# First batch's key and query transposes two rounds later, and the fourth sum of each group behind its first channel products

## The chip, the core and the metric

The kernel runs on one core of a Trainium2 chip. The metric is the device time of one execution in microseconds (us); a comparison uses medians of several executions. The engines that matter are TensorE (PE in the profile, with its weight loads as PEld), VectorE (DVE), ScalarE (ACT), GpSimd (POOL, which here mostly starts loads) and SyncE (SP, which starts transposing transfers and stores). Each engine runs its own instructions in program order; they wait for each other through semaphores.

## The reference

Two stages follow each other. The shapes are batch 8, 12 heads, 448 tokens, head size 64, so a token has 768 channels.

```python
scores = scale * np.matmul(q, k.transpose(0, 1, 3, 2)) - np.log(S)
attn = 1.0 / (1.0 + np.exp(-scores))
x = np.matmul(attn, v)                       # then heads side by side: (8, 448, 768)
h = np.maximum(x.T @ w_tok1, 0.0) @ w_tok2   # tokens mixed, 448 -> 256 -> 448
u = x + h.T
out = u + np.maximum(u @ w_ch1, 0.0) @ w_ch2 # channels mixed, 768 -> 1536 -> 768
```

The attention is a sigmoid without a sum over a row, so a round of scores can be used as soon as its sigmoid is done.

## The kernel before

**Units and groups.** Batches 0 and 1 are the units A and B and are done one at a time; the other six form the groups 1, 2 and 3 of two batches each (lines 73 to 81). A unit has three pairs, a group six; a pair is a set of four heads' worth of rows that fill the 128 partitions. `(A, 1)` is the second pair of unit A.

**A pair's attention** takes seven rounds j = 0 to 6. `scores` (line 442) does four small matmuls into one of two PSUM pair banks, then ACT computes the sigmoid of 128x896 into the tile `attn` (line 456). The two banks alternate, so the matmuls of round n+2 wait until the sigmoid of round n is over. `values_mm` (line 462) multiplies a round's `attn` by the values. For unit A each round's value product comes on its own (`value_step`, line 1404); after j = 6 two DVE casts bring the result to SBUF (line 1412), and then follow, per pair: eight transposes back to rows (`back`, line 500, copy at line 506), eight matmuls of the first token product (`tok1_third`, line 639), and two times two of the second (`tok2_third`, line 671, added by DVE at line 680). The second needs the token weights in order, one DVE copy of 128x896 (line 1355, `tokens_turned`).

**Keys and queries** must be transposed. For the pairs of A, of B and the first of group 1 TensorE does it: `turn_by_pe` (line 369) issues 14 small transposes (line 376) into a free bank of m2 and m3 and one DVE copy of 128x896 (line 381), once for k and once for q. All later pairs are turned by a GpSimd copy and a transposing transfer on SP (lines 363 and 391).

**The channel products.** Units A and B use plain products (lines 887 and 945). A group uses seven products in place of eight for each 2x2 block (as Winograd does): `ch1_pieces` (line 728) has 42 pieces of three matmuls each (line 768), in the order p = 1, 2, 6, 5, 7 of column block 0, then 1 and 2 of block 1, 4 of block 0, 6 of block 1, and 3 of block 0. Pieces 1, 6 and 7 go one after another into the same bank m0, m1 or m2 and each is copied out by DVE before the next is added (`save`, line 783, for group 3 partly by ACT at line 781). Piece 5 reads the sum S1, piece 6 S2, piece 7 S3 and piece 3 S4. `ch1_sum` (line 706) makes them on DVE at line 722 from the transposed rows `uT`; S1 and S2 come in parts, S3 (in place, in `uT`) and S4 as one 128x1344 instruction each.

**What sets the order.** While the program is written, a plan keeps a clock for each engine (`clock`) and the time at which each result will be there (`there`). `first_attention` (line 1347) takes for TensorE, among its candidates, the one that can start first; a tie goes to the one that is listed first: scores, the next entry of `quick` (back and token products), the next entry of `turns` (TensorE's transposes), the copy of the token weights, a value step, then B's rounds. `one` (line 1128) puts the two transposes of the next pair in `turns` after a given round. `merge` (line 1249) does the same for all that follows: channel products in their fixed order (`main`), attention and token work spread between them (`sec`), sums for DVE (`side`). An entry of `side` may be written once the position in `main` has reached its first number; `base[g]` is the position of group g's first piece. Loads from GpSimd are planned by `pool_dma` (line 171): 0.61 an issue, a time of flight, and a cost on a clock of the load path.

Of the kernel before, what the change touches and what calls it, by code (L numbers as in the profile page):

```python
# [21 lines left out]
def kernel(  # L22
# [58 lines left out]
    PAIRS = [(u, i) for u in UNITS for i in range(NPAIR[u])]  # L81
    BY_PE = 7
# [15 lines left out]
    AROUND = ("B", 1, 2, 3)  # L98
    BEHIND = 0.0
    WARM = 9  # L100
    BANKS = ("m0", "m1", "m2", "m3")
    AWAY = 1
    ORDER = (4, 5, 6, 3, 0, 1, 2)
# [22 lines left out]
    clock = {"pe": 1.0, "dve": 1.0, "act": 1.0, "pool": 1.0, "sp": 1.0, "load": 2.4}  # L126
    there, held = {}, set()
# [23 lines left out]
    def did(engine, cost, needs, gives, tail=0.0):  # L151
        t = max([clock[engine]] + [there.get(key, 0.0) for key in needs])
        clock[engine] = t + cost
        for key in gives:
            there[key] = t + cost + tail
            held.discard(key)
        return t
# [12 lines left out]

    def pool_dma(issues, cost, needs, gives):
        did("pool", 0.61 * issues, needs, [])
        clock["load"] = max(clock["load"], clock["pool"] + 1.5) + cost
        for key in gives:
            there[key] = clock["load"] + 0.1

    hook, later = [], []

# [81 lines left out]
    def load_first():  # L260

        got = []
        for n, (j0, j1) in enumerate(KEYS):
            t = pa.tile(
                [128, 2, j1 - j0, E],
                FP16 if n else FP32,
                tag="pk" if n else "h2T",
                bufs=1 if n else 2,
                name=f"k_A_0{n}",
            )  # L270
            for side, (b, h) in enumerate(SIDES["A"]):
                engine = nc.gpsimd if n else nc.scalar if side else nc.sync
                engine.dma_start(
                    out=t[64 * side : 64 * side + 64, :, :, :],
                    in_=k[b, h : h + 2].rearrange("h (p j) e -> p h j e", j=J)[:, :, j0:j1, :],
                )
            got.append(t)
            if n:
                pool_dma(2, 0.2 * (j1 - j0), [], [("made", n)])
            else:  # L280
                did("sp", 0.56, [], [("raw", "A", 0, "k")], 2.9)
                clock["load"] += 0.2 * (j1 - j0)
                load("A", 0, "q")
        return got
# [84 lines left out]
    def turn_by_pe(g, i, what):  # L369
        at = either()  # L370
        t = turned(g, i, what)
        ps = bank(f"t{what}_{g}_{i}", [128, J, 2, P], FP16, at)
        m = raws[(g, i, what)]
        for j in range(J):
            for h in range(2):
                nc.tensor.transpose(  # L376
                    out=ps[64 * h : 64 * h + 64, j, :, :].rearrange("d b p -> d (b p)"),
                    in_=m[:, h, j, :],
                    identity=ident[:, :],
                )  # L380
        nc.vector.tensor_copy(out=t[:, :, :, :], in_=ps[:, :, :, :])
        m = f"m{at}"
        pe(0.42, [("raw", g, i, what), m], ["pe"], "col")
        dve(0.56, ["pe"], [(what, g, i), m])

    def turn_by_dma(g, i):
        for what in ("k", "q"):
            permute(g, i, what)
            m = linear[(g, i, what)]
            t = turned(g, i, what)  # L390
            nc.sync.dma_start_transpose(
                out=t.rearrange("e j b p -> e j (b p)"),
                in_=m.rearrange("p j h e -> p (j h e)"),
            )
            did("sp", 1.4, [("linear", g, i, what)], [(what, g, i)], DMAT)
        if later and later[0][0] <= clock["sp"] + BEHIND:
            later.pop(0)[1]()

    def ahead(g, i, n):
        at = PAIRS.index((g, i)) + n  # L400
        return PAIRS[at] if at < len(PAIRS) else None
# [3 lines left out]
    def load_next(g, i):  # L405


        if not ahead(g, i, 2) or PAIRS.index((g, i)) + 3 < BY_PE + 1:
            return
        def keys():  # L410
            t = state["turned"]
            return [("k", *ahead(g, i, 2))] + ([("uT", t, LAST)] if t is not None else [])

        def f():
            gate = pa.tile([1, 2], FP16, tag="gate", bufs=2, name=f"gate_{g}_{i}")
            last = max(keys(), key=lambda key: there[key])
            if last[0] == "k":
                source = kT[last[1:]][0:1, 0, 0, 0:2]
            else:
                source = uTs[last[1]][0:1, NDB - 1, 128 * LAST : 128 * LAST + 2]  # L420
            nc.gpsimd.tensor_copy(out=gate[:, :], in_=source)  # L421
            did("pool", 0.2, keys(), ["gate"])
            if ahead(g, i, 3):
                load(*ahead(g, i, 3), "k")
                load(*ahead(g, i, 3), "q")
            if PAIRS.index((g, i)) + 2 > BY_PE:
                load(*ahead(g, i, 2), "v")

        loads.append((keys, f))
# [12 lines left out]
    def scores(g, i, j):  # L442
        ps = pair_bank(f"qk_{g}_{i}_{j}", [128, 2, 512])
        at = pa.tile([128, 2, S], FP16, tag="attn", bufs=ATTN, name=f"attn_{g}_{i}_{j}")
        attn[(g, i, j)] = at
        for b in range(2):
            for h in range(2):
                r = slice(64 * h, 64 * h + 64)
                nc.tensor.matmul(  # L449
                    out=ps[64 * b : 64 * b + 64, h, 0:S],  # L450
                    lhsT=keys_of(g, i, j)[r, b, :],
                    rhs=qT[(g, i)][r, :, b, :],
                    start=True,
                    stop=True,
                )
        nc.scalar.activation(  # L456
            out=at[:, :, :], in_=ps[:, :, 0:S], func=SIGMOID, bias=att_bias, scale=att_scale
        )
        pe(0.2, [key_of(g, i, j), ("q", g, i), rot["at"]], ["pe"], "quad")
        act(0.83, ["pe"], [("attn", g, i, j), rot["at"]])  # L460
# [500 lines left out]
    def bank2(p, n):  # L961
        return {2: 3, 5: 2, 3: 2}.get(p, (1, 0, 1)[n])
# [159 lines left out]
    turns, quick, side, base = [], [], [], {}  # L1122
# [5 lines left out]
    def one(g, i, j):  # L1128
        scores(g, i, j)
        at = ahead(g, i, 1)  # L1130
        if j == (3 if (g, i) == ("A", 0) else 1) and at and PAIRS.index(at) < BY_PE:
            for what in ("k", "q"):
                turns.append(
                    ([("raw", *at, what), "m2/m3"], lambda what=what: turn_by_pe(*at, what))
                )
        after = ahead(g, i, 2)
        if j == J - 1 and after and PAIRS.index(after) >= BY_PE:
            keys = [("raw", *after, "k"), ("raw", *after, "q")]
            loads.append((lambda: keys, lambda: turn_by_dma(*after)))
            load_next(g, i)  # L1140
# [108 lines left out]
    def merge(main, sec):  # L1249
# [18 lines left out]
        def free(keys):  # L1268
# [3 lines left out]
            soon = [key for x in main[pos : pos + AWAY] for key in x[2]]  # L1272
            return not any(key in soon for key in keys if key in BANKS)

# [140 lines left out]
    with tc.manual_schedule(engines=None):  # L1415
        if WARM:
            zero = pa.tile([128, 512], FP16, tag="tmp", bufs=4, name="zero")
            nc.vector.memset(zero[:, :], 0.0)
            ps = pp.tile([128, 2, 512], FP32, tag="q1", bufs=1, name="warm")
            for _ in range(WARM):  # L1420
                nc.tensor.matmul(
# [3 lines left out]
        first = load_first()  # L1425
# [13 lines left out]
        load_pair("A", 2)  # L1439
        w_tok2_s = load_tok_weights()  # L1440
        pool_dma(3, 3.7, [], ["wtok"])
        load_pair("B", 0)

# [66 lines left out]
        for g in (1, 2, 3):  # L1510
# [13 lines left out]
            for m in range(42):  # L1524
                p, cb = chain_order(KC)[m]
                at = {2: 3, 5: (cb - 1) % 3, 3: (cb - 1) % 3}.get(p, cb % 3)
# [5 lines left out]
            for m in range(1, 25):  # L1532
# [3 lines left out]
                else:  # L1536
                    n, p = (m - 4) // 7, (1, 2, 6, 5, 7, 3, 4)[(m - 4) % 7]
                    at = bank2(p, n)
# [54 lines left out]
            (3, 0, S, (0, 1, 2), ("S1",), "S3"),  # L1593
        )
        for g in (1, 2, 3):
            first = base[g] - 8
            for m, c0, c1, blocks, after, gives in SUMS:
                needs = [("uT", g, t) for t in blocks] + [(x, g) for x in after]
                side.append(
                    (  # L1600
                        first,
                        first + 1000,
                        needs,
                        lambda g=g, m=m, c0=c0, c1=c1, needs=needs, gives=gives: ch1_sum(
                            g, m, c0, c1, needs, [(gives, g)]
                        ),
                    )
                )
        for m in range(16):
            made = base["B"] + NCB  # L1610
            first = made if m % 4 == 3 else base["A"] + 2
            side.append((first, made + (10 if m % 4 == 3 else 0), ["w1"], w_sum(m)))
        for m in range(12):
            first = base["A"] + NCB + J if m % 4 < 2 else made
# [38 lines left out]
```

## Time and profile before

| quantity | value |
|---|---|
| four runs | 365.4, 365.99, 366.58, 368.55 us; median 366.28 |
| the profiled execution | 365.4 us, of which its span from first to last instruction is 363.6 |
| TensorE | 351.6 us busy (97% of the span), 3113 matmuls |
| VectorE | 232.1 us (64%) |
| ScalarE | 197.5 us (54%) |
| GpSimd | 130.7 us (36%) |
| granted TensorE clock | 0.996 of full speed |

The profiled execution is the fastest of the four, and the runs spread by 3.15 us, which is 0.9%. A "wait" in the profile is idle time of an engine with the instruction that ended it. The chain of waits goes back from the last instruction, at each step to whatever released it. The table by stretches gives the busy time of each engine between two moments, so that the difference from the stretch's length is idle time. In a line of the timeline the first number is the start and the second the length in us; lines that follow each other closely can overlap by the time that a matmul takes to drain.

### The profile page before, as it was taken

To read this page: it belongs to the slowest core of one execution; us is meant where nothing else is said; L and a number is where in the kernel's file an instruction comes from. 1 tells how busy PE (TensorE), PEld (TensorE's weight loads), DVE (VectorE), ACT (ScalarE), POOL (GpSimd) and SP (SyncE) were. 2 spreads that over 40 slices of the span, in tenths; PEclk is the share of its full clock that TensorE was granted. 3 is DMA by queue.
4 is the path that set the end of the run, shared out by engine and by line. 5 is a ranking of instruction groups with operands and counts; after the bars stand their busy time and mean duration, and the time that the engine had idled before them with its cause. 6 is when DMAs were issued, how large, how long until landed. Compare 5 with 4: busy or idle time off the path is not lost.

```text
span 363.6 us, 7773 instructions
## 1 busy us (share of the span) xinstructions
PE 351.6 (97%) x3113; PEld 182.5 (50%) x3113; DVE 232.1 (64%) x435; ACT 197.5 (54%) x242; POOL 130.7 (36%) x211
## 2 busy tenths in 40 slices
PE   7899999999999999999999999999999999999994
PEld 3454555555544556444445556444445556455562
DVE  2467757666755588886654659666644588655862
ACT  4987266466765432387887743477887351342000
POOL 9982422465556610055655340066610000004000
PEclk9999999999999999999999999999999999999998
DMA  7999999689998946798999889998963158300153
GB/s 113 187 192 192 148 208 183 103 127 160 161 147 134 138 73 107 191 154 133 147 146 140 144 172 127 219 138 133 142 103 70 52 89 180 92 2 0 45 159 103
DMA packets 86725, 47.76 MB, mean 131 GB/s; under 512 B 60961, under 2 KB 82977, under 8 KB 86689
## 3 DMA queue, kind: packets, MB, share of 16 engines
q0 software_dynamic: 24288, 21.83, 41.3%
q1 hardware_dynamic: 61696, 23.96, 34.1%
q10 hardware_dynamic: 704, 1.48, 1.1%
q8 instruction: 24, 0.39, 0.4%
q14 instruction: 13, 0.10, 0.1%
HBM read 43.84 MB, written 11.01 MB: 151 GB/s over the span
## 4 chain that ended last, share of the span: by engine, by line
PE 89%; ACT 3%; DVE 2%; POOL 1%; DMA 1%; issue 1%; ACTq 0%; POOLq 0%
PE x L768 12%; PE x L1031 9%; PE qk L449 9%; PE xa L467 7%; PE z L768 6%; PE c_B L945 4%; PE z L1031 4%; PE k L538 4%; PE c_B L887 4%; PE yn L574 4%; PE c_A L887 4%; PE c_A L945 3%; PE d L1088 3%; PE y L1031 2%; PE y L768 2%; ACT attn_A L456 2%
## 5 line engine op out<-in xcount | busy, mean ns | idle before, releaser
L456 ACT ACTIVATE attn<-qk 128x896 f16<-128x896 f32 x126 | 110.5, 915 | 54.4 <-PE qk L449 47.1
L768 PEld LDWEIGHTS <-w 128*128 128x128 f16 x378 | 35.0, 98 | 39.1 <-issue 9.8
L449 PE MATMUL qk<-qT,kT 64*64 64x448 f16 x504 | 40.8, 363 | 0.6 <-ACT attn L456 0.6
L783 DVE COPY c<-x 128x448 f32<-128x448 f32 x42 | 26.1, 622 | 22.2 <-PE x L768 19.5
L768 PE MATMUL x<-uT,w 128*128 128x448 f16 x162 | 37.8, 353 | 0.1
L788 DVE CUSTOM_DVE_ANT_0 h2T<-z,c 128x448 f16<-128x448 f32 x36 | 22.5, 625 | 16.9 <-PE z L768 14.7
L224 ACT ACTIVATE u<-u 128x768 f16<-128x768 f32 x21 | 17.7, 844 | 24.7 <-DVE u L584 21.0
L252 POOL DMA_DIRECT2D k<-in_k_dram x36 | 21.4, 602 | 25.6 <-PE tk L376 12.1
L1043 DVE TENSOR_TENSOR u<-u,x 128x384 f32<-128x384 f32 x36 | 19.9, 552 | 16.3 <-PE x L1031 16.2
L1031 PEld LDWEIGHTS <-h2T 128*128 128x128 f16 x216 | 20.8, 98 | 15.0 <-issue 1.6
L363 POOL COPY pk<-k 128x896 f16<-128x896 f16 x17 | 16.3, 958 | 30.8 <-DMA k<-in_k_dram 30.8
L449 PEld LDWEIGHTS <-kT 64*64 64x64 f16 x504 | 13.7, 104 | 27.0 <-issue 25.1
L467 PE MATMUL xa<-attn,v 64*64 64x448 f16 x504 | 27.0, 350 | 0.0
L421 POOL COPY gate<-kT 1x2 f16<-1x2 f16 x16 | 2.8, 174 | 67.0 <-DMA kT<-pk 67.0
L456 ACT ACTIVATE attn_B<-qk_B 128x896 f16<-128x896 f32 x21 | 18.3, 917 | 15.4 <-PE qk_B L449 14.9
L768 PE MATMUL z<-s,w 128*128 128x448 f16 x108 | 24.6, 353 | 0.0
L688 POOL TENSOR_TENSOR r<-h2T,h2T 128x512 f16<-128x512 f16 x1 | 1.1, 1150 | 60.1 <-ACT h2T L236 60.1
L584 DVE TENSOR_TENSOR u<-x_nat,yn 128x384 f32<-128x384 f16 x42 | 21.2, 550 | 2.3 <-PE yn L574 2.1
L252 POOL DMA_DIRECT2D v<-in_v_dram x36 | 22.2, 644 | 0.3 <-issue 0.3
L252 POOL DMA_DIRECT2D q<-in_q_dram x36 | 21.8, 624 | 0.3 <-issue 0.2
L1031 PEld LDWEIGHTS <-r 128*128 128x128 f16 x162 | 15.5, 98 | 11.0 <-issue 1.2
L1031 PE MATMUL x<-w_s,h2T 128*128 128x384 f16 x108 | 20.5, 326 | 0.1
(140 smaller groups left out, 623.2 us busy)
## 6 DMA issues: line engine op xcount, KB each, us to landing
out_dram<-u SPq DMA_DIRECT2D x49, 192.0 KB, 3.0
k<-in_k_dram POOLq DMA_DIRECT2D x36, 112.0 KB, 4.2
q<-in_q_dram POOLq DMA_DIRECT2D x36, 112.0 KB, 4.6
v<-in_v_dram POOLq DMA_DIRECT2D x36, 112.0 KB, 4.8
w<-in_moe_w_ch_dram POOLq DMA_DIRECT2D x2, 1152.0 KB, 11.9
w<-in_moe_w_ch_dram POOLq DMA_DIRECT2D x1, 2304.0 KB, 22.7
out_dram<-u ACTq DMA_DIRECT2D x7, 192.0 KB, 3.4
q_A<-in_q_dram POOLq DMA_DIRECT2D x6, 112.0 KB, 4.3
```

What stands on the lines that cost most here:

```text
L252: nc.gpsimd.dma_start(out=t[64 * side : 64 * side + 64, :, :, :], in_=src[b, h + 2 * i : h + 2 * i + 2].rearrange("h (p j) e -> p h j e", ...
L449: nc.tensor.matmul(out=ps[64 * b : 64 * b + 64, h, 0:S], lhsT=keys_of(g, i, j)[r, b, :], rhs=qT[(g, i)][r, :, b, :], start=True, stop=True,)
L456: nc.scalar.activation(out=at[:, :, :], in_=ps[:, :, 0:S], func=SIGMOID, bias=att_bias, scale=att_scale)
L467: nc.tensor.matmul(out=ps[b][64 * h : 64 * h + 64, :], lhsT=vf[r, h, j, :], rhs=attn[(g, i, j)][r, h, :], start=(j == 0), stop=(j == J - 1),)
L584: nc.vector.tensor_tensor(out=u_of(g, t)[:, DH * half : DH * half + DH], in0=x_of(g, half)[:, t, :], in1=ps[:, half, 0:DH], op=ADD,)
L768: nc.tensor.matmul(out=ps[:, :], lhsT=W(p, n, cb), rhs=A[p](n), start=(first and n == 0), skip_group_check=True, stop=(n == KD - 1),)
L783: nc.vector.tensor_copy(out=s[:, :], in_=bk[(cb, "x")][:, :])
L788: nc.vector._custom_dve(dve_ops.TENSOR_ADD_SAT, out=h[half][:, cb, S * b : S * b + S], in0=ps[:, :], in1=snap[(cb, n)][:, :], s0=BIG, s1=0.0,)
L887: nc.tensor.matmul(out=bk[cb][:, :], lhsT=w1[:, n, 128 * cb : 128 * cb + 128], rhs=uTs[g][:, n, OFF[g] : OFF[g] + S], start=(n == 0), stop ...
L945: nc.tensor.matmul(out=o, lhsT=h2T[b][:, cb, c], rhs=w2[:, cb, DH * half : DH * half + DH], start=(cb == 0), stop=(cb == NCB - 1),)
L1031: nc.tensor.matmul(out=ps[:, :], lhsT=A(p, n, kb), rhs=W(p, kb), start=(first and kb == 0), skip_group_check=True, stop=(kb == KC - 1),)
L1043: nc.vector.tensor_tensor(out=u, in0=u, in1=ps[:, :], op=ADD)
```

## The change

Three constants are new, and three places use them.

- `TURN`: the transposes of the next pair go into `turns` after round 3 for all three pairs of A. Before it was round 3 for the pair (A, 0) and round 1 for (A, 1) and (A, 2).
- `LAND`: the plan puts the arrival of a GpSimd load 1.7 behind the load path's clock in place of 0.1, and the path starts 1.0 behind the issue in place of 1.5. This alters no instruction, only the times that the plan reckons with.
- `S4_AT`: the sum S4 of a group may be written from position `base[g] + 3`, behind its pieces 1, 2 and 6 of block 0, and not from `base[g] - 8` on as the other sums.

```diff
@@ -98,6 +98,9 @@
     AROUND = ("B", 1, 2, 3)
     BEHIND = 0.0
     WARM = 9
+    S4_AT = 3
+    LAND = 1.7
+    TURN = {("A", 0): 3, ("A", 1): 3, ("A", 2): 3}
@@ -170,9 +173,9 @@
     def pool_dma(issues, cost, needs, gives):
         did("pool", 0.61 * issues, needs, [])
-        clock["load"] = max(clock["load"], clock["pool"] + 1.5) + cost
+        clock["load"] = max(clock["load"], clock["pool"] + 1.0) + cost
         for key in gives:
-            there[key] = clock["load"] + 0.1
+            there[key] = clock["load"] + LAND
@@ -1128,7 +1131,7 @@
     def one(g, i, j):
         scores(g, i, j)
         at = ahead(g, i, 1)
-        if j == (3 if (g, i) == ("A", 0) else 1) and at and PAIRS.index(at) < BY_PE:
+        if j == TURN.get((g, i), 1) and at and PAIRS.index(at) < BY_PE:
             for what in ("k", "q"):
                 turns.append(
                     ([("raw", *at, what), "m2/m3"], lambda what=what: turn_by_pe(*at, what))
@@ -1593,8 +1596,8 @@
         for g in (1, 2, 3):
-            first = base[g] - 8
             for m, c0, c1, blocks, after, gives in SUMS:
+                first = base[g] + (S4_AT if m == 4 else -8)
                 needs = [("uT", g, t) for t in blocks] + [(x, g) for x in after]
```

## The prediction

> **What bounds the kernel now.** I read the page first, then the chain of waits, then TensorE's waits, then the stretches around the places that the change touches.
>
> ```profile
> PE 351.6 (97%) x3113; PEld 182.5 (50%) x3113; DVE 232.1 (64%) x435; ACT 197.5 (54%) x242; POOL 130.7 (36%) x211
> PE 89%; ACT 3%; DVE 2%; POOL 1%; DMA 1%; issue 1%; ACTq 0%; POOLq 0%
> ```
>
> TensorE is busy for 351.6 of 363.6 us and holds 89% of the chain. The change takes no matmul away, so all that it can win or lose is TensorE's idle time, 12.0 us in all. A table by stretches, cut where the chain changes hands, says where that lies (start and end, length, then each engine's busy time):
>
> ```profile
> 5.00:12.20 7.20, 5.49 (x97) 3.28 (x100) 1.96 (x4) 4.75 (x6) 7.20 (x13) 1.00 1.11 153
> 12.20:20.40 8.20, 6.88 (x121) 3.56 (x117) 3.25 (x6) 8.15 (x10) 6.39 (x12) 1.00 1.19 195
> 20.40:27.80 7.40, 7.40 (x104) 4.18 (x108) 5.88 (x11) 5.17 (x7) 6.92 (x12) 1.00 1.20 191
> 27.80:36.00 8.20, 7.50 (x100) 3.73 (x96) 6.36 (x13) 6.79 (x8) 1.51 (x4) 1.00 1.18 196
> 36.00:146.00 110.00, 109.99 (x1063) 57.91 (x1056) 72.62 (x128) 58.64 (x67) 47.68 (x75) 1.00 0.86 140
> ```
>
> TensorE's idle time is 1.71 us up to 12.2, 1.32 up to 20.4, nothing up to 27.8, 0.70 up to 36, and 0.01 in the next 110 us. In the second row ACT is the full engine, 8.15 of 8.20: the sigmoids of A's rounds set the pace there. From 36 on the starts of the three groups show gaps (0.31 at 150.3, 0.43 at 231.3, some 0.26 around 310), the groups' insides a few tenths, and after the last product at 358.2 come 5.4 us of addition and store. Since TensorE never catches up with anything in between, a gap that closes anywhere shortens the whole by its length.
>
> **S4 behind the first pieces.** The chain at the starts of groups 1 and 2 (start, length, engine and line):
>
> ```profile
> 148.66 0.56 DVE u L955
> 149.22 0.77 DVE s L722
> 149.99 0.54 DVE c L783
> 150.53 0.04 issue
> 150.57 0.73 PE x L768 x3
> ```
>
> ```profile
> 229.39 0.85 DVE u L1043 x2
> 230.25 0.85 DVE s L722
> 231.09 0.55 DVE c L783
> 231.64 0.04 issue
> 231.68 0.73 PE x L768 x3
> ```
>
> VectorE does S4 (0.85) and only then the copy of piece 1, which frees the bank for piece 6. In TensorE's timeline the gap before piece 6 is smaller than S4, because eight score matmuls stand in between:
>
> ```profile
> 150.57 0.73 PE L768 MATMUL x<-s,w 128*128 128x448 f16 x3 [0.31 <-DVE c L783]
> 231.68 0.73 PE L768 MATMUL x<-s,w 128*128 128x448 f16 x3 [0.43 <-DVE c L783]
> ```
>
> With S4 gone from there the copy starts when the addition before it is over, at 149.22 instead of 149.99, and ends near 149.85; TensorE is occupied with scores until 150.26. So the gap goes wholly: 0.31. In group 2 likewise: copy from 230.25 to 230.8, scores until 231.25, 0.43 saved. What is late next is nothing on TensorE: piece 5 needs S1, which has long been there. In group 3 the copies of pieces 1 and 6 are ACT's (0.55 each, they make both small gaps there), VectorE isn't in the way, and I count nothing. Sum: 0.74 less.
>
> S4 has to be paid at its new place. The rules let it come after piece 6's copy, and its reader, piece 3, stands six pieces further on, which with the 28 value matmuls in between is some 6 us later. In group 2 VectorE rests 2.44 us before 235.58, in group 3 1.43 before 312.61: both hold 0.85. In group 1 it does four weight sums there (0.55 each, from 151.88 to 154.08), with 0.56 idle behind them; the sums that S4 displaces are for the second products, from 188 on. If that cover is gone and the next copy comes 0.85 late, piece 4 or 6 of the next block waits about as long as piece 6 did, and the win of that group is given back.
>
> The Trainium skill, "SBUF — State Buffer", section "Who interferes with whom", speaks against the new place: a VectorE instruction with two inputs in SBUF blocks a GpSimd instruction that reads SBUF, for the whole instruction. S4 is such a one. In the trace GpSimd's next reader, the one-element gate copy, starts at 153.02 in group 1 and 236.39 in group 2, after waits of 23.26 and 19.71 for a transfer, so no overlap is to be seen here; by the page the worst would be 0.85 on a queue of loads that TensorE doesn't wait for, and the sum stays the same.
>
> **The first batch: what moves.** LAND makes the plan expect each load 1.1 later (+1.6 in arrival, -0.5 in start, when GpSimd's issue is the limit). The first query load is the first thing that the plan waits for, so the sigmoids are planned some 1.1 later too, and the order of A's first pair should stay as it is, with the 0.56 wait for the keys of (A, 1):
>
> ```profile
> PE tk_A L376 <- DMA k_A<-in_k_dram: 0.6, 1, 0.6
> ```
>
> TURN does alter the order. Two times 14 transposes (0.51 of TensorE each, as in the chain's row "25.49 0.51 PE tq_B L376 x14") and their copies (0.62 each) of the pair (A, 2) now stand at 14.34 and 15.35, after rounds 1 and 2 of (A, 1); they become eligible after round 3. In their stead come the last value step and its two casts (1.15), about 0.6 to 1 us sooner, which bring no end nearer since the token product waits for other rounds. By the rules' order and the trace's durations: rounds 2 and 3 start when their banks are free (some 14.8 and 15.6, before 15.06 and 15.86), then the eight back-transposes (0.55), then the keys' 14, from about 16.4 to 16.9, right where round 4 is due. ACT runs eleven sigmoids from 12.25 to 21.40 with 0.83 each; round 4's would start at 17.24, and its scores now end at about 17.3 to 17.5. Cost: 0 (if the scores win the tie) to 0.25 us on the pace that counts here. I take 0.2. The queries' 14 come after round 5, near 17.6; their copy stands behind those of the back-transposes (0.69) and of the keys (0.62) and ends about 18.9; the first round of (A, 2) is due before 19.74, so 0.4 is left after its 0.38 of scores.
>
> Unit B's first pair keeps its turn to round 3 of (A, 2) either way, but by the ties' order its keys and then its queries are now taken before the order copy of the token weights (0.87) and before the token products. In the trace the queries' 14 stand at 25.42, and ACT then rests 2.31 until B's first sigmoid:
>
> ```profile
> 28.29 3.35 ACT L456 ACTIVATE attn_B<-qk_B 128x896 f16<-128x896 f32 x4 [2.31 <-PE qk_B L449]
> 35.76 1.52 PE L467 MATMUL xa_B<-attn_B,v_B 64*64 64x448 f16 x28 [0.29 <-ACT attn_B L456]
> ```
>
> With the queries some 2 us earlier B's rounds start earlier, and the two gaps in which TensorE waits for B's sigmoids (0.39 at 29.7, 0.29 at 35.5) can shrink; the first token products come 1 us later in exchange. The trace shows no such order. The bounds are 0.7 won (both gaps) and 0.6 lost (a wait like the 0.29 and another, in the stretch that has none now). I take 0.35 won, half of the gaps, being nearer to those rows.
>
> **LAND later on.** From 36 us on it may reorder SP's queue: transposing transfers of keys and queries (1.22 us each) planned 1.1 later can fall behind stores. GpSimd's own order doesn't change, since its entries are taken one after the other. The cover is that keys are turned about a pair ahead, 8 us or more. From none to one such transfer ahead of a group's first piece, 0 to 1.2; I take 0.2.
>
> **Sum.** -0.74 + 0.2 - 0.35 + 0.2 = -0.7 us. From the profiled execution's 365.4 that is 364.7; it was the fastest of the four runs, and the median is 366.28. On that I put it: 365.6 us, 0.2% less. About 1% is what a measurement of this kernel can tell from no change, so this is within it.
>
> **Rivals.**
> 1. *The wait only moves* (0.15): S4 in front of another copy, or the weight sums pushed behind it, gives the 0.74 back and the batch is a draw. For it: VectorE is 85% busy around group 1's start (5.09 of 6.00 us). Against it: the idle time in groups 2 and 3. Time 366.3.
> 2. *The late queries starve ACT, and it is slower* (0.14). Place: the change from (A, 1) to (A, 2). If the queries' 14 are taken only after round 6, whose matmuls end at 18.65: 18.65 + 0.51 + 0.51 for both transposes, 0.72 for the copy and its signal, 0.4 for scores is 20.8, against 19.74: 1.1 us without a sigmoid, TensorE having only values to do. It decides from 0.9 us on, where it eats the rest of the sum. With 1.1 in place of my 0.2 the whole is +0.2, with B's part lost too +0.55, and with B's lower bound +1.15: 366.5 to 367.4, in the middle 366.9. Against it: 28 value matmuls of (A, 1) alone can't fill the time before round 6, so the transposes should get in.
> 3. *B runs ahead* (0.13): both B gaps and the 0.56 wait for keys go as well, -0.74 - 0.7 - 0.56 = -2.0: 364.3.
> 4. *The plan's shifted times reorder the rest* (0.10): each of the 5 later transitions of unit or group gets a wait like the 0.56 or a transfer's 1.22: 3 to 6 us, 369 to 372. For it: 0.01 us of idle in 110 leaves nothing to win there, only to lose. Against: the engines' slack, DVE 66% and ACT 53% in that row.
> The forecast has 0.48.
>
> **How the numbers follow.** Chances: faster by over 1% (below 362.6) needs 3.7 of the 12 us of idle time, of which 6.6 lie at the very start and end: 0.04. Slower by over 1% (above 369.9): rival 4's greater part, 0.08. Within: 0.88. The range leaves out rival 4 and the far end of rival 3 and takes in the runs' own spread: 363.4 to 368.2.
>
> **What would show it.** After: no S4 between the addition and the copy of piece 1 in groups 1 and 2, piece 6 straight after the scores; TensorE's waits at L768 for the copy L783 gone; 14 transposes for (A, 2) at about 16.4 and 17.6; ACT's eleven sigmoids still close together but for some 0.2; B's first sigmoid before 28.29. I am wrong if ACT shows a gap of 0.9 or more near 20, or if TensorE's waits grow in the stretch from 36 to 146.

## The result, and the profile after

The changed kernel takes 365.52 us (median of 44 runs, 364.86 to 367.43) against 366.51 for the kernel before (70 runs beside it). The ratio is 0.9975 with a 95% interval of 0.9966 to 0.9985: 0.92 us less, between 0.55 and 1.25. The forecast was 365.6. So it is faster, by a quarter of one per cent. The profiled execution of the changed kernel ran for 365.58 us with a span of 363.8, so it was an ordinary one, while that of before (365.40) was the fastest of its four.

From the page of the changed kernel: busy time by engine, and the chain of work that ended last by engine.

```profile
PE 351.8 (97%) x3113; PEld 182.8 (50%) x3113; DVE 234.0 (64%) x435; ACT 197.6 (54%) x242; POOL 131.8 (36%) x211
...
PE 92%; ACT 3%; DVE 1%; DMA 1%; issue 1%; POOL 0%; ACTq 0%; POOLq 0%; DVEq 0%
```

TensorE's share of the chain went from 89% to 92% and VectorE's from 2% to 1%. The lines of the profile stand 3 further down: L768 is now L771, L783 is L786, L449 is L452, L722 is L725.

The table by stretches, with the cuts of the prediction (start, end and length, then busy time of PE, PEld, DVE, ACT and POOL, the granted clock, the DMA share and GB/s):

```profile
5.00:12.20 7.20, 5.32 (x75) 2.84 (x74) 1.67 (x3) 3.91 (x6) 7.20 (x14) 0.76 1.15 162
12.20:20.40 8.20, 6.85 (x130) 4.04 (x130) 3.63 (x6) 7.76 (x10) 6.10 (x12) 1.00 1.19 193
20.40:27.80 7.40, 7.16 (x108) 3.70 (x104) 5.34 (x10) 6.41 (x8) 7.40 (x12) 1.00 1.20 191
27.80:36.00 8.20, 7.87 (x105) 4.25 (x93) 6.40 (x13) 6.27 (x8) 2.68 (x5) 1.00 1.19 198
36.00:146.00 110.00, 109.70 (x1065) 57.98 (x1065) 71.60 (x126) 59.27 (x68) 47.43 (x74) 1.00 0.87 138
```

Fixed cuts mislead here, for the first row has a granted clock of 0.76, where before had 1.00: this execution reached the pair (A, 1) 0.94 us late, and everything behind it is shifted. Another profiled execution of the same changed kernel has no such stretch and the same stages behind it (but for 0.18 in one), so this is scatter of the start and not the change. I therefore compare stages by TensorE's own marks, from the start of one named matmul to the start of another. All of these are differences of start times in the traces:

| stage, us | before | after | difference |
|---|---|---|---|
| (A, 1)'s first scores to A's first token product | 7.12 | 7.39 | +0.27 |
| to B's first value matmul | 15.43 | 15.14 | -0.29 |
| to A's first second product | 36.61 | 36.61 | 0 |
| to group 1's piece 1 (the former 72 to 148) | 76.09 | 75.74 | -0.35 |
| group 1's pieces | 37.58 | 37.28 | -0.30 |
| group 1's second products and the rest to group 2 | 43.41 | 43.41 | 0 |
| group 2's pieces | 37.46 | 37.35 | -0.11 |
| to the last matmul | 90.97 | 90.96 | -0.01 |
| sum | 344.67 | 343.88 | -0.79 |

The sum is what the prediction said, -0.7. Its terms are not: the gaps in front of piece 6 gave 0.41 and not 0.74, and the stretch that was to lose 0.2 to LAND won 0.35.

What became of the gap at group 1's start. First the chain of waits of the changed kernel between 146 and 156 (start, length, engine, line):

```profile
150.32 0.50 PE qk L452 x8
150.83 0.69 PE x L771 x3
151.51 0.02 issue
151.54 0.63 DVE c L786
152.17 0.04 issue
152.21 0.73 PE x L771 x3
```

Then the timeline of VectorE and TensorE there:

```profile
149.35 0.55 DVE L958 TENSOR_TENSOR u<-u,c_B 128x384 f32<-128x384 f32 x1
149.82 0.62 DVE L786 COPY c<-x 128x448 f32<-128x448 f32 x1
...
150.76 0.74 PE L771 MATMUL x<-s,w 128*128 128x448 f16 x3
...
151.34 0.73 PE L771 MATMUL z<-s,w 128*128 128x448 f16 x3
151.54 0.62 DVE L786 COPY c<-x 128x448 f32<-128x448 f32 x1 [0.34 <-PE x L771]
152.08 0.85 DVE L725 TENSOR_TENSOR s<-uT,s 128x1344 f16<-128x1344 f16 x1
152.21 0.73 PE L771 MATMUL x<-uT,w 128*128 128x448 f16 x3
```

The copy of piece 1 now follows the addition at once (149.82), and piece 6 starts at 150.76, straight behind the scores. S4 starts at 152.08, behind the copy of piece 6, and nobody waits for it. But a new wait stands one step on. Before, a score round and 28 value matmuls stood between piece 5 (`z`) and piece 7, which uses piece 6's bank again. Now piece 7 comes directly behind piece 5, and piece 6's copy, which frees that bank, lasts till 152.16. The step from piece 5's last matmul to piece 7 takes 0.50 where a step between such matmuls takes 0.19: 0.31 lost again. In group 2 it takes 0.57, which is 0.38 lost, and the list of TensorE's waits names a part of it:

```profile
PE x L771 <- DVE c L786: 0.2, 1, 0.2
```

### The profile page after: what moved, and what is told of

Read it like the earlier page. It is cut to its first block, busy times and chain, and to the rows that moved or that the text cites. A ratio compares the mean times of both kernels' runs of the same rounds, so it can differ in the third digit from the quotient of the medians.

```text
span 363.8 us, 7774 instructions
## 1 busy us (share of the span) xinstructions
PE 351.8 (97%) x3113; PEld 182.8 (50%) x3113; DVE 234.0 (64%) x435; ACT 197.6 (54%) x242; POOL 131.8 (36%) x211
## 4 chain that ended last, share of the span: by engine, by line
PE 92%; ACT 3%; DVE 1%; DMA 1%; issue 1%; POOL 0%; ACTq 0%; POOLq 0%; DVEq 0%
PE x L771 12%; PE x L1034 9%; PE qk L452 9%; PE xa L470 7%; PE z L771 5%; PE z L1034 5%; PE c_B L948 4%; PE k L541 4%; PE c_B L890 4%; PE c_A L890 4%; PE yn L577 4%; PE c_A L948 3%; PE d L1091 3%; PE y L771 3%; PE y L1034 2%; PE qk_B L452 1%
## 5 line engine op out<-in xcount | busy, mean ns | idle before, releaser
L771 PEld LDWEIGHTS <-w 128*128 128x128 f16 x378 | 34.8, 98 | 39.0 <-issue 9.9
L452 PE MATMUL qk<-qT,kT 64*64 64x448 f16 x504 | 40.9, 363 | 0.6 <-ACT attn L459 0.6
L786 DVE COPY c<-x 128x448 f32<-128x448 f32 x42 | 26.2, 623 | 21.1 <-PE x L771 19.5
L771 PE MATMUL x<-uT,w 128*128 128x448 f16 x162 | 37.8, 353 | 0.5 <-DVE c L786 0.2
L1046 DVE TENSOR_TENSOR u<-u,x 128x384 f32<-128x384 f32 x36 | 19.9, 552 | 16.4 <-PE x L1034 16.2
L227 ACT ACTIVATE u<-u 128x768 f16<-128x768 f32 x21 | 17.7, 843 | 22.5 <-DVE u L587 15.7
L452 PEld LDWEIGHTS <-kT 64*64 64x64 f16 x504 | 13.7, 104 | 27.0 <-issue 25.4
L366 POOL COPY pk<-k 128x896 f16<-128x896 f16 x17 | 16.5, 968 | 27.5 <-DMA k<-in_k_dram 27.4
L771 PE MATMUL z<-s,w 128*128 128x448 f16 x108 | 24.6, 353 | 0.0
L366 POOL COPY pq<-q 128x896 f16<-128x896 f16 x17 | 16.3, 960 | 16.9 <-DMA q<-in_q_dram 15.2
```

The source lines that it names most:

```text
L366: nc.gpsimd.tensor_copy(out=m[:, :, :, :], in_=raws[(g, i, what)].rearrange("p h j e -> p j h e"))
L452: nc.tensor.matmul(out=ps[64 * b : 64 * b + 64, h, 0:S], lhsT=keys_of(g, i, j)[r, b, :], rhs=qT[(g, i)][r, :, b, :], start=True, stop=True,)
L771: nc.tensor.matmul(out=ps[:, :], lhsT=W(p, n, cb), rhs=A[p](n), start=(first and n == 0), skip_group_check=True, stop=(n == KD - 1),)
L786: nc.vector.tensor_copy(out=s[:, :], in_=bk[(cb, "x")][:, :])
```

## The experiments

**The three parts, each alone, and the whole beside them.** Each alone is the kernel before with one part of the diff. S4 alone:

```diff
-            first = base[g] - 8
             for m, c0, c1, blocks, after, gives in SUMS:
+                first = base[g] + (3 if m == 4 else -8)
```

> Only the sum S4 moves; TURN and LAND are as before, so TensorE's order differs in the groups 1 and 2 alone. Theory A (the gap closes and the next one opens): the gaps of 0.31 and 0.43 before piece 6 go, but TensorE, now ahead of the sigmoids, takes piece 7 early and waits 0.2 to 0.3 for the copy of piece 6, in each of the two groups; net 0.3 to 0.5 us less, ratio 0.9986 to 0.9992. Theory B (the prediction's sum): the whole 0.74 less, ratio 0.998, and no wait at piece 7. Theory C (the gain is the plan's new order of loads): 1.000 and group starts that are no earlier.

TURN alone:

```diff
-        if j == (3 if (g, i) == ("A", 0) else 1) and at and PAIRS.index(at) < BY_PE:
+        if j == {("A", 0): 3, ("A", 1): 3, ("A", 2): 3}.get((g, i), 1) and at and PAIRS.index(at) < BY_PE:
```

> Only TURN; the order differs from before in the first 45 us alone. Theory A: the late transposes of (A, 2) cost 0.2 to 0.3 us up to A's first token product, and unit B's earlier queries give the same back before its first value products: 0 within 0.15, ratio 0.9995 to 1.0005. Theory B (the prediction): 0.15 less, ratio 0.9996. Rival (ACT starves at the change of pairs): 0.4 or more longer, ratio over 1.001, with an ACT gap of 0.9 near 20 us.

LAND alone:

```diff
-        clock["load"] = max(clock["load"], clock["pool"] + 1.5) + cost
+        clock["load"] = max(clock["load"], clock["pool"] + 1.0) + cost
         for key in gives:
-            there[key] = clock["load"] + 0.1
+            there[key] = clock["load"] + 1.7
```

> Only LAND; TensorE's order is that of before up to 72 us and from 148 us on, and differs between, where A's second products and B's products stand with group 1's scores. Theory A: 0.3 to 0.4 us less between the first of A's second products and group 1's first piece, ratio 0.999. Theory B (the prediction, which saw only the transfers' order): 0 to 1.2 longer, I took 0.2, ratio 1.0005. If the 0.35 that the two profiles show there is scatter, the ratio is 1.000.

The change itself, beside its parts:

> The change as it is, on the same chip as its parts. Ratio 0.9975 as measured. Theory A: it is the sum of the three parts, some 0.4 + 0 + 0.35 = 0.75 to 0.9 us less, and the late first query load (0.69) and the half clock from 8.6 to 12.0 us in the first profile of it are scatter, so that another profile begins like that of before: first scores near 6.9. Rival: they belong to the change, and the first scores come at 7.5 again.

Against 366.17 us for the kernel before, in five rounds:

| kernel | median, us | ratio | 95% interval | that is, us |
|---|---|---|---|---|
| S4 alone | 365.29 | 0.9974 | 0.9958 to 0.9990 | -0.95 (-1.54 to -0.37) |
| TURN alone | 366.15 | 0.9993 | 0.9978 to 1.0009 | -0.26 (-0.81 to +0.33) |
| LAND alone | 366.03 | 0.9989 | 0.9974 to 1.0004 | -0.40 (-0.95 to +0.15) |
| the change | 365.31 | 0.9966 | 0.9951 to 0.9981 | -1.24 (-1.79 to -0.70) |

Of the parts, only S4's time differs from that of before by more than its interval. The traces tell more, because most stages that a part doesn't touch agree to 0.02 us between executions. The stages of S4 alone come from an execution of its own, of 367.12 us:

> Only S4 moves, for its profile (the profiled execution of the first look was disturbed, 1223 us, and says nothing). Theory A: the order up to group 1's first piece is that of before, so the time there differs only by how the first loads land; in groups 1 and 2 piece 6 comes straight behind the scores (gaps of 0.3 to 0.7 gone) and piece 7 starts 0.2 to 0.3 behind piece 5. Group 1's first to group 2's first piece: 80.6 to 80.7 us, against 80.99 before. Theory B: 80.6 and no wait at piece 7.

Here are the stages in which anything differs (us, as in the table above); the two kernels in the last rows come further below.

| kernel | (A, 1) to token product | to B's values | 72 to 148 | group 1 | group 2 |
|---|---|---|---|---|---|
| before | 7.12 | 15.43 | 76.09 | 37.58 | 37.46 |
| the change | 7.39 | 15.14 | 75.74 | 37.28 | 37.35 |
| S4 alone | 7.12 | 15.43 | 76.09 | 37.28 | 37.60 |
| TURN alone | 7.39 | 15.14 | 76.09 | 37.58 | 37.56 |
| LAND alone | 7.12 | 15.43 | 75.80 | 37.58 | 37.72 |
| TURN later still | 7.60 | 14.92 | 76.02 | 37.58 | 37.45 |
| S4 twice | 7.12 | 15.43 | 76.09 | 38.23 | 38.34 |

What follows: the parts separate cleanly. TURN moves 0.27 from one side of the first token product to the other and wins nothing. Of what the two sides are made, the busy time between the same marks tells. Up to the first token product TensorE is busy for 6.25 us in both kernels, and its idle time grows from 0.87 to 1.14. From there to B's values its idle time falls only from 0.70 to 0.63, for the wait of 0.39 for B's sigmoid is gone, but a new one stands near its place. The eight transposes back now wait for VectorE's addition of the second token product (from the changed kernel):

```profile
31.88 0.61 PE L503 MATMUL xb_A<-ident,uT_A 128*128 128x128 f16 x8 [0.33 <-DVE uT_A L683]
```

The other 0.22 of the 0.29 is TensorE's busy time, 14.51 for 14.73, for the same matmuls in another order. LAND shows nothing of its own but 0.29 less in 72 to 148. S4 shortens group 1 by 0.30. In group 2 its effect hangs on the execution: the gap before piece 6 was 0.43 in the profile of before, 0.5 in TURN alone and 0.7 in LAND alone, whose orders are the same there. So the profile of before, the fastest of its four runs, shows the gap at its smallest. Over all profiles, group 2's pieces take 37.45 to 37.72 in the five executions with S4 once at its old place (before, TURN, LAND and, further below, TURN later still and the tile last), and 37.35 or 37.36 in four of the five with S4 at its new place and the order of the pieces unchanged. That fits a timed gain of S4 that lies above the 0.41 of the two profiles, but its interval takes in 0.41 as well. In S4 alone, group 2's 37.60 contains 0.25 of another origin. Up to 256 us its steps are those of the change, and then a score round waits for ACT, which itself had waited for a transfer. ACT's row in that trace:

```profile
255.95 0.92 ACT L227 ACTIVATE xT<-xa 128x896 f16<-128x896 f32 x1 [0.89 <-DMA x_nat<-xT]
```

**S4 twice at its old place.** Is VectorE's work in front of the copy passed on to TensorE one to one?

```diff
-        nc.vector.tensor_tensor(out=o, in0=x, in1=y, op=op)
+        for _ in range(2 if m == 4 else 1):
+            nc.vector.tensor_tensor(out=o, in0=x, in1=y, op=op)
```

> The kernel before, with S4 done twice at its old place (the same sum into the same tile; 0.77 more of VectorE per group, from start to start). If that place is on the path, each of the groups 1 and 2 loses the whole 0.77, 1.5 us in all, ratio 1.004, and group 3, whose copies are ACT's, nothing or little. If the copy of piece 1 had other cover, 0 to 0.5 us, ratio under 1.0015.

Measured: 367.60 us against 366.61, ratio 1.0032 (1.0012 to 1.0051), 1.17 us more (0.44 to 1.87). In the trace, group 1 grows by 0.65 and group 2 by 0.88, and group 3 not at all. Its timeline at group 1's start:

```profile
149.46 1.74 DVE L723 TENSOR_TENSOR s<-uT,s 128x1344 f16<-128x1344 f16 x2
...
151.12 0.62 DVE L784 COPY c<-x 128x448 f32<-128x448 f32 x1
151.79 0.73 PE L769 MATMUL x<-s,w 128*128 128x448 f16 x3 [1.20 <-DVE c L784]
```

The gap before piece 6 grows from 0.31 to 1.20, by more than the second S4's 0.77 from start to start, and 0.2 of that comes back at the value matmuls that had waited for ACT behind it. So S4 did sit on the path, nearly one to one. Taken away, it gives less than added, because the next limit is only a step behind.

**Piece 1 of block 1 in front of piece 7.** If the wait at piece 7 is all that the change leaves lying there, filling it with another piece should bring it in. On the changed kernel, at the end of the list of pieces in `chain_order`:

```diff
+        seq[4], seq[5] = seq[5], seq[4]
         return seq + [(4, n - 1), (3, n - 1)]
```

> The change, and in each group's first block piece 1 of the next block in front of piece 7, so that the copy of piece 6 lies beside a product. Theory A (the next wait is the copy of piece 6): the 0.2 to 0.3 before piece 7 goes in groups 1 and 2 and 0.13 in group 3, up to 0.6 less than the change, ratio to the kernel before 0.995 to 0.9965. Rival: it moves on once more, to the copy of the next block's piece 1 or to the sigmoids, and the ratio is that of the change, 0.9966 to 0.9975.

Measured: 366.48 us against 366.61, ratio 0.9997 (0.9977 to 1.0017). The gain of the change is gone. TensorE's timeline:

```profile
150.78 0.73 PE L771 MATMUL z<-s,w 128*128 128x448 f16 x3
151.35 0.73 PE L771 MATMUL x<-uT,w 128*128 128x448 f16 x3
152.01 0.38 PE L452 MATMUL qk<-qT,kT 64*64 64x448 f16 x4
...
155.12 0.85 PE L452 MATMUL qk<-qT,kT 64*64 64x448 f16 x8
```

The wait at 152.2 is filled, as meant. Further on, eight scores take 0.85 where they took 0.57, since they wait for a sigmoid. TensorE's waits on ACT in groups 1 and 2 double from 0.3 to 0.6 each. Together with the second products the two groups take 0.59 and 0.80 more than in the change (81.28 and 80.24 against 80.69 and 79.44). Of that, 0.44 and 0.63 are idle time of TensorE, and the changes of the weights' shape, whose price comes below, are as many as in the change (44 and 42). So the wait at piece 7 is not simply unfilled time; the score rounds around it are held by ACT as well.

**The transposes later still.** Rival 2 of the prediction by itself: the transposes of the pair after (A, 1) only behind round 6, on the kernel before.

```diff
-        if j == (3 if (g, i) == ("A", 0) else 1) and at and PAIRS.index(at) < BY_PE:
+        if j == {("A", 0): 3, ("A", 1): 6}.get((g, i), 1) and at and PAIRS.index(at) < BY_PE:
```

> The kernel before, with the transposes of (A, 2) eligible only after round 6 of (A, 1); they then stand together behind that round's scores, and the scores of (A, 2) behind them. The prediction's second rival: ACT without a sigmoid for 1.1 us near 20, and as much longer in all, ratio 1.003. If TensorE's later work absorbs it (unit B's rounds come earlier, as with TURN), the loss at A's first token product is 1.1 but under 0.5 in all, ratio under 1.0015.

Measured: 366.27 us against 366.61, ratio 0.9994 (0.9974 to 1.0014). ACT's timeline:

```profile
11.24 8.50 ACT L459 ACTIVATE attn_A<-qk_A 128x896 f16<-128x896 f32 x10 [0.75 <-PE qk_A L452]
20.80 3.35 ACT L459 ACTIVATE attn_A<-qk_A 128x896 f16<-128x896 f32 x4 [1.07 <-PE qk_A L452]
24.32 2.54 ACT L459 ACTIVATE attn_A<-qk_A 128x896 f16<-128x896 f32 x3 [0.17 <-PE qk_A L452]
27.59 1.73 ACT L459 ACTIVATE attn_B<-qk_B 128x896 f16<-128x896 f32 x2 [0.73 <-PE qk_B L452]
```

The gap that rival 2 described is there and has its size, 1.07 against 1.1. It costs TensorE 0.48 up to the first token product, and the next stage gives 0.51 back. From (A, 1)'s first scores to B's first values it is 22.55 us before, 22.53 with TURN and 22.52 with TURN later still. Within these, TensorE's idle time rises, 1.57, 1.77 and 2.00, and its busy time falls by about as much, 20.98, 20.76 and 20.52. From one order to the next the weights' shape changes less often, 29, 27 and 24 times, which makes 0.11 and 0.09 us of busy time for each change that is saved, near the price that is measured next. Why the two sides balance so closely no run here shows.

**What a change of shape costs.** LAND's 0.29 in 72 to 148 had no wait to come from, since the list of TensorE's waits is empty there before and after the change. What differs is where B's mixed token tile stands. From TensorE's timeline of the kernel before (the last two numbers of a shape such as 128\*64 are the weights' rows and columns):

```profile
129.90 0.82 PE L574 MATMUL yn<-h1T,w_tok_n 128*128 128x384 f16 x4
130.65 0.35 PE L945 MATMUL c_B<-w,h2T_A 128*64 128x384 f16 x1
130.65 0.35 PE L945 MATMUL c_B<-w,h2T_B 128*64 128x384 f16 x1
130.84 0.33 PE L945 MATMUL c_B<-w,h2T_A 128*64 128x384 f16 x1
130.84 0.33 PE L945 MATMUL c_B<-w,h2T_B 128*64 128x384 f16 x1
131.10 0.82 PE L574 MATMUL yn<-h1T,w_tok_n 128*128 128x384 f16 x4
```

And of the changed kernel:

```profile
133.85 0.81 PE L577 MATMUL yn<-h1T,w_tok_n 128*128 128x384 f16 x4
134.50 0.49 PE L948 MATMUL c_B<-w,h2T_B 128*128 128x384 f16 x2
134.82 0.81 PE L577 MATMUL yn<-h1T,w_tok_n 128*128 128x384 f16 x4
```

From the token products to the next kind it is 0.75 before (129.90 to 130.65) and 0.65 after (133.85 to 134.50), with four matmuls in both. Before, the neighbours have 128x64 weights, and after, they have 128x128. So I measured the change of shape by itself, with extra matmuls of 384 columns on zeros behind the warm-up (in `grouped`, 12 of one shape and then 12 of the other; in `in turn`, one of each, 12 times):

```diff
+            for f in [full] * 12 + [half] * 12 + [full, half] * 12:
+                f()
+            for f in [full] * 12 + [quad] * 12 + [full, quad] * 12:
+                f()
```

> The kernel before with 88 extra matmuls of 384 columns on zeros behind the warm-up: 16 of 128x128 to get up to the clock, then 12 of 128x128, 12 of 128x64 and 24 that alternate between the two; then the same with 64x64 in place of 128x64. Theory (a change of the weights' shape costs TensorE time of its own, read from the traces as 0.258 in place of 0.163 us from start to start): in the two grouped runs every step is 0.16 except the one at the change, in the alternating ones every step is about 0.26, so 24 alternating matmuls take about 2.2 us more than 24 grouped ones, with either shape. Rival (the 0.1 is a wait of the neighbours, for a bank or for weights, that the profile doesn't name): the alternating steps are 0.16 as well. The total is longer by the extra work, some 17 us, and says nothing.

Its timeline of TensorE, at the border from grouped to in turn (L1426 has 128x128 weights, L1431 128x64, L1436 64x64):

```profile
9.46 2.14 PE L1431 MATMUL warm<-zero 128*64 128x384 f16 x12
11.53 0.34 PE L1426 MATMUL warm<-zero 128*128 128x384 f16 x1
11.80 0.35 PE L1431 MATMUL warm<-zero 128*64 128x384 f16 x1
12.08 0.34 PE L1426 MATMUL warm<-zero 128*128 128x384 f16 x1
...
22.24 0.34 PE L1426 MATMUL warm<-zero 128*128 128x384 f16 x1
22.50 0.35 PE L1436 MATMUL warm<-zero 64*64 64x384 f16 x1
22.78 0.34 PE L1426 MATMUL warm<-zero 128*128 128x384 f16 x1
```

Within a group, each matmul starts 0.163 after the one before. In turn, the steps are 0.267 and 0.282 with 128x64, and 0.266 and 0.279 with 64x64. Twenty-four in turn take 6.59 us (11.53 to 18.12) and twenty-four grouped take 4.11 (7.42 to 11.53), a difference of 2.47 against the 2.2 expected. A change of the weights' shape costs 0.10 to 0.12 us, and no wait is shown for it; the granted clock is 1.00 from 5 to 28.6 us. The two shapes also write to two different banks, but that is not the price: in group 1 of the kernel before, pieces 1 and 2 go to different banks with one shape, and the step from one to the other (148.46 to 149.03 for three matmuls) is 0.19 like the others. The Trainium skill, "TensorEngine Tiling (Array Packing)", section "Key Properties", says that changing the tiling mode drains TensorE; it gives no figure. This run fits that and has a figure, 0.10 to 0.12 us, though it shows a longer step and not what TensorE does in it. The prediction had not used that rule.

**The mixed tile last.** If it is the shapes, the same gain is to be had without LAND. On the kernel before, in `ch2_single_order`:

```diff
-        blocks = (0, 1, 2) if g == "A" else (MIXED, 4, 5, 6)
+        blocks = (0, 1, 2) if g == "A" else (4, 5, 6, MIXED)
```

> The kernel before with nothing but B's mixed token tile put last in place of first among B's second products, so that its 128x64 products no longer stand between the 128x128 token products. The plan then has about 10 changes of shape fewer in the block from 72 to 148. Theory of the shapes (0.095 a change): this block shrinks by 0.5 to 0.95 us, with no wait gone, and the total comes to 365.2 to 365.7 beside 366.2 to 366.6 of before. Rival (what LAND won there came from the planned arrival times, not from the shapes): nothing here, within 0.2.

The same line in the changed kernel, and on the kernel before together with S4's new place:

> The changed kernel with B's mixed token tile last as well. LAND has already taken the tile out from between the token products there, so the plan has only 2 changes of shape fewer than the change: theory of the shapes: 0 to 0.2 less than the change, 1.0 to 1.2 less than before. If the two gains were independent, as the rival has it, it would be 0.5 to 0.95 less than the change.

> The kernel before with S4 at its new place and B's mixed token tile last, without LAND and TURN. If S4 and the shapes are all that the change wins, this is as fast as the change or faster by up to 0.5: 0.9 to 1.5 less than before. If LAND or TURN win something that the shapes don't stand for, it is slower than the changed kernel with the tile last.

Against 366.34 us for the kernel before. The changes of shape are counted in TensorE's timeline, from one group of matmuls to the next:

| kernel | median, us | ratio | 95% interval | 72 to 148, us | changes of shape there |
|---|---|---|---|---|---|
| before | 366.34 | | | 76.09 | 48 |
| LAND alone (from above) | | | | 75.80 | 44 |
| the change (from above) | | | | 75.74 | 44 |
| before, tile last | 365.56 | 0.9981 | 0.9961 to 1.0001 | 75.40 | 42 |
| the change, tile last | 365.14 | 0.9961 | 0.9938 to 0.9984 | 75.59 | 42 |
| S4 and tile last | 365.53 | 0.9978 | 0.9961 to 0.9994 | 75.46 | 42 |

By its time, the tile last alone is just not told from the kernel before. By its trace it wins 0.69 in that stretch (0.63 together with S4, in the same order) with six changes fewer, 0.105 to 0.115 each, which is the price that the extra matmuls showed; LAND's four stand for 0.29, 0.07 each. The two are not independent: on top of the change it wins only 0.15 more. The count doesn't explain everything, since two orders with 42 changes differ by 0.13 to 0.19. S4 and the tile last measured 0.81 less than before, where 0.9 to 1.5 was expected if S4 and the shapes are all. Its median lies above that of the change with the tile last, but the stages don't show it: from (A, 1) on they differ by 0.12 in favour of S4 and the tile last, and the intervals overlap. The changed kernel with the tile last has the lowest median of all, but against the change itself no difference is shown.

## Why the prediction was right or wrong

- **The bound.** Right in the main: TensorE holds the chain. But idle time was not all that there was to win. A busy TensorE can be slower by the order of its shapes, and this I had ruled out ("all that it can win or lose is TensorE's idle time", and in rival 4 "leaves nothing to win there, only to lose").
- **S4, -0.74.** The mechanism was right: VectorE's S4 kept the copy of piece 1, and both gaps before piece 6 went. S4's new place cost nothing; its reader didn't wait. The step that failed is "What is late next is nothing on TensorE". I looked at piece 5, which is indeed free, and not at piece 7 behind it, which needs the bank that piece 6's copy frees. Nor did I expect the score round and value matmuls that had stood between them to go behind piece 7. From start to start, the step to piece 6 fell by 0.37 and 0.49, and the step to piece 7 rose by 0.31 and 0.38. In group 1 some 0.2 in front of the value matmuls went as well, which by the sigmoids' times was a wait for ACT. So 0.41 remained of 0.74 (0.30 and 0.11 in the stages). I had also taken the gaps of one execution, the fastest, as their size; group 2's gap was 0.43 to 0.7 in kernels that have the same order there.
- **TURN, +0.2.** It measured +0.27, just above the bound of 0.25. The transposes came where I put them: their 14 start at 17.44 and 18.65, which is 16.5 and 17.7 without the late start, against 16.4 and 17.6. ACT's gap from the late round 4 is 0.30, and all of the 0.27 is idle time of TensorE, as the term had it.
- **B's earlier queries, -0.35.** It measured -0.29, but not for the reason given. The term was half of B's two gaps. One of them went and the other stayed, and the new wait of 0.33 for VectorE, which the prediction doesn't have, took the place of the one that went; the waits together gave 0.07. The other 0.22 is TensorE's own time in another order, of which the change of shape that is saved there can be only a part. That the size came out is luck. Relative to (A, 1), B's first sigmoid comes 0.71 sooner (14.37 behind its first scores in place of 15.08), though not before 28.29 on the clock of this execution, as I had written. With TURN later still the two terms cancel again, at nearly twice the size (+0.48 and -0.51), waits on one side and TensorE's own time on the other; why they balance stays open.
- **LAND, +0.2.** Wrong in sign and in kind. I looked for its effect in SP's queue; what it reordered was TensorE's, in B's second products, and it won 0.29 alone and 0.35 with the rest. Four changes of shape fewer, at the measured price, are enough for that; that nothing else has a part in it is not shown.
- **The sum, -0.7.** -0.79 in the profiles and -0.92 (0.55 to 1.25) by time. It came out right by luck: S4's 0.33 too much and LAND's 0.55 too little, with 0.13 missing from the first batch, nearly cancel. The forecast was met, and half of its reasons were not.
- **The rivals.** Rival 1, "the wait only moves", was half the truth: about half of the gain moved to piece 7. Rival 2's gap in ACT exists when it is provoked, with 1.07 for the 1.1 that I had worked out, but its price for the total was wrong: TensorE lost 0.48 by it and got 0.51 back before B's values, by orders with fewer changes of shape as far as the count tells. Rival 3 is not seen: of B's two gaps the 0.39 went, but the 0.29 before its values is still there (0.3 in the list of waits), and a new one of 0.33 came. Rival 4 is not seen as a loss; the reordering happened, and it won.
- **The page's rule on shared ports** that spoke against S4's new place had nothing to act on: S4 runs from 152.08 to 152.93 in group 1 and from 232.84 to 233.69 in group 2, and GpSimd's next copies start at 155.71 and 236.76.

## What to carry to other kernels

When a wait for a freed bank goes, follow the same bank one use further, and look at what the order puts between the two uses: the gain is the distance to that next wait, not the length of the gap. In a stretch in which TensorE is always busy, count the places where the weights' shape changes; at the 0.10 to 0.12 us that the extra matmuls showed, 48 of them are an estimated 5 us of a 76 us stretch, and no list of waits shows them. A gap that closes is not yet time won, since another can open beside it, as B's 0.39 and 0.33 show. A gap is no constant, either: take it from several executions before it goes into a sum.

## What the hardware showed that I had not expected

- A change of the weights' shape costs 0.10 to 0.12 us, whether to 128x64 or to 64x64, as the extra matmuls showed. The step from the first pieces to a score round, 0.28 against 0.19, has nearly the same extra.
- Early in some executions the granted clock falls to half for some 3.4 us, once, between 7 and 14 us: in the changed kernel it is 0.91 from 7 to 9 us, 0.50 from 9 to 11, 0.74 from 11 to 13 and 1.00 before and behind. The profiles of TURN, LAND and S4 alone and of the tile last have such a stretch too, and those of before and of the changed kernel's other execution don't. From the first scores to (A, 1) it is 6.35 to 6.63 us without it and 6.28 to 7.44 with it, so that up to some 0.9 us of the scatter between executions may come from there; the stage also holds waits for loads. What sets it off was not tried.
